# First mixture-of-experts layer computed over groups of 3, 3, 4 and 3 token tiles, with the first weights stationary

## Chip, cores, metric

The kernel runs on one core of one Trainium2 chip. The metric is the device time of one execution in microseconds (us). Before the change it is 708.86 us, the median of three runs (708.36 to 709.52).

## What is computed

Three layers follow each other. Attention over 2 x 8 heads of 768 tokens and width 64, masked by a hash bucket, gives 1536 tokens of width 512. Then a mixture of experts:

```python
logits = x @ w_gate + modality_bias[modality_id]      # x (1536, 512), 8 experts
e_idx = np.argmax(logits, axis=1)
gate_w = softmax(logits)[arange(N), e_idx]
for e in range(E):
    mask = e_idx == e
    h = np.maximum(x[mask] @ w1[e], 0.0)              # w1 (8, 512, 1024)
    out[mask] = gate_w[mask, None] * (h @ w2[e])      # w2 (8, 1024, 512)
```

and a second layer `h = x @ w_in; g = max(h,0) + alpha*min(h,0); g @ w_out` with inner width 2048, called the second mixture here. Everything is 32-bit. The matrix products of both mixtures are done in three terms: each operand is split into a rounded high part and the rest (high x high, rest x high, high x rest).

## The kernel before, in words

The order of every instruction is written out by hand; each engine runs its own list in that order.

**Routing.** The 768 tokens of the first batch are routed while attention still runs. Their most frequent expert fills three tiles of 128 tokens (`NPRE = 3`) ahead of time. The rest of the routing (`Router.S`, `R`, `adjust`, `GATE`, `place`, `experts`, `tokens`, `slots`, `slots2`), a row of small VectorE operations, runs after attention, between the matrix products of those first three tiles. `experts` writes the expert of each tile, whether it differs from the tile before, and the number of tiles. 13 tiles (`NBASE`) are always computed; tiles beyond are computed in `rest`, under a branch on the number.

**One tile t.** `TX` transposes the 128 gathered tokens (4 TensorE transposes) and splits them into high and rest (one ScalarE and one VectorE operation). `G1` makes two halves of 128 tokens x 512 hidden columns: the tokens are stationary, the weights `w1h`, `w1l` move, 12 matmuls of 512 columns a half; ScalarE evicts each half through a relu into `hr`. `TH` transposes the hidden tile (8 transposes) and splits it on ScalarE (`hh`) and VectorE (`hl`). `G2` makes 24 matmuls of 512 columns into `y`; `Y` scales by the gate on ScalarE and writes the tile to DRAM (`ys`). PSUM has 2 buffers for `G1` (`pg`), 3 for transposes (`ptr`), 2 for `y` and 1 for the router (`rps`).

**Weights.** SyncE loads the 4 MB of an expert for every tile (`load1`: `r1`, two halves of w1; `load2`: `r2`, w2). Where the expert changed, `W1s` and `W2` split them on ScalarE (high) and VectorE (rest), under a branch. For the first three tiles, the first layer's weights are split during the last steps of attention and those of the second layer by `W2()` after it.

**Around it.** `hook(s)` puts work between the attention steps: at step 96 tile 0 is transposed, at steps 98 and 100 the first half of its `G1` runs. During the main loop over tiles 3 to 12 the weights of the second mixture are loaded (`CL`) and repaired from 64-bit words (`CV`, five parts, the first on ScalarE, four on VectorE; all share one staging buffer), and the router's `dense`, `dense2` compute where each token's row lies in `ys`. At the end `GY` gathers rows of `ys`, `TY` transposes them, and the second mixture begins.

Of the kernel before, what the change touches and what calls it, by code (L numbers as in the profile page):

```python
# [35 lines left out]
LAGS = (0, 0)  # L36
ORDER = "aVDNmbnefopAL"
# [7 lines left out]
NBASE = 13  # L45
ELD = 88
# [8 lines left out]
class Router:  # L55
# [5 lines left out]
    def constants(self, w_gate, mbias, mod):  # L61
# [60 lines left out]
        yield  # L122

# [257 lines left out]
    def experts(self):  # L381
# [12 lines left out]
        v.tensor_tensor(out=a, in0=a, in1=self.iota[0:1, 0:8].unsqueeze(1).to_broadcast(s), op=ALU.mult)  # L394
        et = self.tmp([1, NT], F32, "et")
        v.tensor_reduce(out=et, in_=a, axis=AX.X, op=ALU.add)
        v.tensor_copy(et[:, 0:NPRE], self.es[0:1].to_broadcast([1, NPRE]))
# [3 lines left out]
        tt = self.tmp([1, 1], F32, "ttt")  # L401
        v.tensor_reduce(out=tt, in_=nt[0:1, 0], axis=AX.X, op=ALU.add)
        v.tensor_scalar(out=info[:, 2 * NT:2 * NT + 1], in0=tt, scalar1=float(NPRE), scalar2=None, op0=ALU.add)
# [52 lines left out]
    def dense2(self, ps):  # L456
        nc = self.nc
        v = nc.vector
        HD, rv = self.dn
        p = ps()  # L460
        for c in range(12):
            nc.tensor.matmul(p[:, 0:36], HD[:, c], rv[:, c].rearrange("p a t -> p (a t)"), start=(c == 0), stop=(c == 11))
        t = self.tmp([128, 3, 12], F32, "dt")
        v.tensor_copy(t, p[:, 0:36].rearrange("p (a t) -> p a t", a=3))
        v.tensor_copy(self.did, t[:, 0])
        v.scalar_tensor_tensor(out=self.dpos, in0=t[:, 2], scalar=128.0, in1=t[:, 1], op0=ALU.mult, op1=ALU.add)
# [7 lines left out]
def _program(base, tc, nc, q, k, v, proj, mod, w_gate, mbias, w1, w2, win, wout, alpha, out):  # L474
# [6 lines left out]
    ys = dram.tile([NT * 128, 512], F32, tag="ys", name="ys")  # L481
# [21 lines left out]
    def hook(s):  # L503
# [11 lines left out]
        if 74 <= s < 74 + NT - NBASE:  # L515
            t = NBASE + s - 74
# [34 lines left out]
        if s == 96:  # L551
            z = slot16(0)
            h, lo = R["x0"] = z[:, 0:512], z[:, 512:1024]
            p = misc()
            for kk in range(4):
                nc.tensor.transpose(p[:, kk * 128:kk * 128 + 128], xg[0][:, kk * 128:kk * 128 + 128], ident)
            nc.scalar.activation(h, p, AF.Copy)
            nc.vector.tensor_tensor(out=lo, in0=p, in1=f32(h), op=ALU.subtract)
        if s in (98, 100):
            h, lo = R["x0"]  # L560
            w1h, w1l = R["w1"]
            if s == 98:
                R["g0"] = GP()
            p = R["g0"]
            for kk in range(s - 98, s - 96):
                ks = slice(kk * 128, kk * 128 + 128)
                for n, (a, b) in enumerate(((h, w1h), (lo, w1h), (h, w1l))):
                    nc.tensor.matmul(p, a[:, ks], b[:, kk, 0:512], start=(kk == 0 and n == 0), stop=(kk == 3 and n == 2))
            if s == 100:
                R["hr0"] = BIG[0][:, 1536:2048]  # L570
                nc.scalar.activation(R["hr0"], p, AF.Relu)
# [395 lines left out]
    def rps():  # L967
        return prt.tile([128, 512], F32, tag="rps", name="rps")

    def trp():  # L970
        return ptr.tile([128, 512], F32, tag="tr", name="tr")

# [30 lines left out]
    xhl, hr, hhl, yps, gps = {0: R["x0"]}, {}, {}, {}, {}  # L1003

    def TX(t):
        p = ptr.tile([128, 512], F32, tag="tr", name="tr")
        for kk in range(4):
            nc.tensor.transpose(p[:, kk * 128:kk * 128 + 128], xg[t][:, kk * 128:kk * 128 + 128], ident)
        if t < NBASE:
            h = mp.tile([128, 512], F32R, tag="xh", name="xh", bufs=2)  # L1010
            lo = mp.tile([128, 512], F32R, tag="xl", name="xl", bufs=2)
        else:
            h, lo = R["xr"][:, 0], R["xr"][:, 1]
        act.activation(h, p, AF.Copy)
        dve.tensor_tensor(out=lo, in0=p, in1=f32(h), op=ALU.subtract)
        xhl[t] = (h, lo)

    def G1(t, half, k0=0, k1=4):
        h, lo = xhl[t]
        if half == 0 and k0 == 0:  # L1020
            h_ = mp.tile([128, 1024], F32, tag="hr", name="hr", bufs=2)
            hr[t] = h_[:, 0:512], h_[:, 512:1024]
        hs = slice(half * 512, half * 512 + 512)
        if k0 == 0:
            gps[t] = pg.tile([128, 512], F32, tag="g", name="g")
        p = gps[t]
        for kk in range(k0, k1):
            ks = slice(kk * 128, kk * 128 + 128)
            for n, (a, b) in enumerate(((h, w1h), (lo, w1h), (h, w1l))):
# [476 lines left out]
```

## Time and profile before

| | |
|---|---|
| median of three runs | 708.86 us |
| the profiled execution, device time | 711.61 us |
| its span, first to last instruction | 709.8 us |
| TensorE busy | 676.0 us, 95% |
| VectorE busy | 443.1 us, 62% |
| ScalarE busy | 331.8 us, 47% |
| mean granted TensorE clock | 0.982 of 2.4 GHz |

PE is TensorE's matmul, PEld its weight load, DVE is VectorE, ACT ScalarE, POOL GpSimd, SP SyncE. L1030 is line 1030 of the kernel. A matmul's duration contains its latency, and the next one begins before it ends; what a matmul costs in a row of them is the distance from start to start. Time in microseconds unless marked ns; clock times are counted from the start of the span. Attention ends at about 258 us, the first mixture at 429 us.

### The profile page before, as it was taken

Reading aid. Unit: us, or ns where it says so; the run is one execution under the profiler, and the core shown is the slowest. Engines: PE = TensorE matmul, PEld = TensorE weight load, DVE = VectorE, ACT = ScalarE, POOL = GpSimd, SP = SyncE. Lnnn points to the kernel's source line nnn. Section 1 sums busy time; section 2 is a strip of 40 time slices with the busy share of each in tenths; the row PEclk is TensorE's granted clock in tenths of the full one; section 3 lists DMA queues with packets and bytes.
Section 4 is the critical chain, followed back from the end, with each engine's and each line's share of the span. In section 5 each row is a group of like instructions: output and inputs, shape, how many; then the busy total and the mean of one; then the engine's idle time right before and its main releaser. Section 6 shows DMA issues by size and latency. Waiting matters only on the chain. (4 is left out here: it accounts for less than half of the span.)

```text
span 709.8 us, 13037 instructions
## 1 busy us (share of the span) xinstructions
PE 676.0 (95%) x4970; PEld 562.3 (79%) x4970; DVE 443.1 (62%) x905; ACT 331.8 (47%) x561; POOL 237.2 (33%) x208
## 2 busy tenths in 40 slices
PE   7799999999989889999999989999999999999996
PEld 6588898998878768788888767788888888888884
DVE  6878788889887768316724557999643344434332
ACT  5577687787867754234533337666311111111111
POOL 8777889998857400210100022021021000110002
PEclk9989999999999899999999999999999999999999
DMA  8375863874624141316522374443011010010001
GB/s 211 92 192 120 187 157 77 182 216 93 136 98 169 43 162 62 109 30 247 199 90 75 89 259 147 128 134 133 1 46 44 1 30 0 16 44 1 1 0 59
DMA packets 31420, 72.41 MB, mean 102 GB/s; under 512 B 7116, under 2 KB 7206, under 8 KB 31094
## 3 DMA queue, kind: packets, MB, share of 16 engines
q1 hardware_dynamic: 28260, 61.81, 30.9%
q0 software_dynamic: 2960, 9.70, 4.1%
q8 instruction: 40, 0.66, 0.4%
q14 instruction: 30, 0.25, 0.1%
q10 hardware_dynamic: 130, 0.00, 0.0%
HBM read 79.15 MB, written 12.06 MB: 128 GB/s over the span
## 5 line engine op out<-in xcount | busy, mean ns | idle before, releaser
L836 POOL TENSOR_TENSOR El<-E,Eh 128x768 f16<-128x768 f32 x88 | 144.4, 1652 | 40.0 <-ACT Eh L835 21.5
L831 ACT ACTIVATE E<-st 128x384 f32<-128x384 f32 x192 | 89.2, 491 | 61.2 <-PE st L830 57.5
L798 DVE TENSOR_REDUCE mx<-mxp 128x1 f32<-128x384 f32 x192 | 97.6, 547 | 10.5 <-PE mxp L797 9.7
L585 ACT ACTIVATE gh<-gf 128x512 fp32r<-128x512 f32 x48 | 30.3, 630 | 143.9 <-PE o L1351 133.4
L835 ACT ACTIVATE Eh<-E 128x768 f16<-128x768 f32 x94 | 79.5, 846 | 0.0
L829 PE MATMUL st<-op 97*128 97x384 f32 x192 | 74.8, 389 | 2.5 <-DMA op<-mr 1.9
L797 PE MATMUL mxp<-op 76*128 76x384 f32 x192 | 66.3, 359 | 6.9 <-ACT E L831 3.2
L588 DVE TENSOR_TENSOR gl<-gf,gh 128x512 fp32r<-128x512 f32 x48 | 33.1, 689 | 60.0 <-ACT gh L585 57.9
L1053 PE MATMUL y<-op,hh 128*128 128x512 f32 x208 | 69.7, 402 | 0.2 <-DVEq L1262 0.2
L1325 PE MATMUL h<-big,op 128*128 128x512 f32 x256 | 68.5, 396 | 0.0
L1368 POOL DMA_INDIRECT out_dram<-x,did x12 | 11.8, 985 | 169.2 <-DVE x L1365 89.8
L830 PE MATMUL st<-op 128*128 128x384 f32 x192 | 67.4, 351 | 0.0
L1351 PE MATMUL o<-op,gh 128*128 128x512 f32 x192 | 64.2, 395 | 0.0
L1030 PE MATMUL g<-op,xh 128*128 128x512 f32 x192 | 62.5, 397 | 1.1 <-PEq L1110 0.6
L846 PE MATMUL av<-vh,El 128*128 128x65 f16 x576 | 59.0, 196 | 2.0 <-POOL El L836 1.9
L844 PE MATMUL av<-vh,Eh 128*128 128x65 f16 x576 | 59.7, 197 | 0.0
L845 PE MATMUL av<-vl,Eh 128*128 128x64 f16 x576 | 59.2, 195 | 0.0
L844 PEld LDWEIGHTS <-Eh 128*128 128x128 f16 x576 | 53.1, 99 | 7.6 <-issue 6.4
L1325 PEld LDWEIGHTS h<-big,op 128*128 128x128 f32 x256 | 48.1, 188 | 11.6
L846 PEld LDWEIGHTS <-El 128*128 128x128 f16 x576 | 53.7, 99 | 2.2 <-POOL El L836 2.2
L845 PEld LDWEIGHTS <-Eh 128*128 128x128 f16 x576 | 53.8, 100 | 0.0
L1207 POOL DMA_INDIRECT yg<-ys,dpos x10 | 12.9, 1287 | 120.6 <-DVE x L1163 65.4
(406 smaller groups left out, 1502.2 us busy)
## 6 DMA issues: line engine op xcount, KB each, us to landing
r<-in_moe_w_dram SPq DMA_DIRECT2D x42, 1024.0 KB
op<-B SPq DMA_DIRECT2D x32, 192.0 KB
op<-in_moe_w_in_dram SPq DMA_DIRECT2D x6, 1024.0 KB
op<-A SPq DMA_DIRECT2D x28, 192.0 KB
op<-A SPq DMA_DIRECT2D x13, 384.0 KB
op<-in_moe_w_out_dram SPq DMA_DIRECT2D x4, 1024.0 KB
ys<-ysb SPq DMA_DIRECT2D x13, 256.0 KB
big<-in_q_dram SPq DMA_DIRECT2D x17, 192.0 KB
```

The lines of the kernel that those rows point to most:

```text
L797: mm(p[:,0:384],t[0:76,2,c*128:(c+1)*128],t[0:76,1,a*384:a*384+384],start=True,stop=True)
L798: nc.vector.tensor_reduce(out=mx[h][:,c,a:a+1],in_=p[:,0:384],axis=AX.X,op=ALU.max)
L829: mm(p[:,0:384],t[0:97,1,js],t[0:97,2,qs],start=True,stop=False)
L830: mm(p[:,0:384],t[:,0,js],t[:,3,qs],start=False,stop=True)
L831: nc.scalar.activation(E[s][0][:,qs],p[:,0:384],AF.Exp,scale=0.125)
L835: else: nc.scalar.activation(eh,e,AF.Copy)
L836: (nc.vector if s>=ELD else nc.gpsimd).tensor_tensor(out=el,in0=e,in1=eh,op=ALU.subtract)
L844: mm(a[:,c*65:c*65+65],eh[:,cs],VH[h//4%2][:,j,h%4,:],start=(j==0 and c==0),stop=False,skip_group_check=True)
L845: mm(a[:,c*65:c*65+64],eh[:,cs],VL[h//4%2][:,j,h%4,:],start=False,stop=False,skip_group_check=True)
L846: mm(a[:,c*65:c*65+65],el[:,cs],VH[h//4%2][:,j,h%4,:],start=False,stop=False,skip_group_check=True)
L1053: nc.tensor.matmul(yps[t], a[:, ks], b[:, kk], start=(kk == 0 and n == 0), stop=(kk == 7 and n == 2))
L1325: nc.tensor.matmul(p, terms[t][0][:, kk, cs], terms[t][1][:, kk], start=(n == 0), stop=(n == 11))
```

## The change

The 13 tiles become four groups of 3, 3, 4 and 3. In a group, `G1(key, c)` makes one chunk of 128 hidden columns for all the group's tokens: 128 columns of w1 are stationary, the tokens move (384 or 512 columns), 12 matmuls a chunk, 8 chunks. Its output has the hidden columns on the partitions already, so `TH` goes. ScalarE evicts the chunk through a relu as high part, VectorE makes the rest from the same PSUM tile. `G2(key, c)` adds one chunk to all the group's `y`. `Y` alternates between ScalarE and VectorE. PSUM: 2 buffers for `G1`, 4 for `y`, 2 for transposes and router together.

The expert's weights are loaded once for a group. `experts` works on 128 partitions and adds six operations that tell whether every group has one expert and the tiles are at most 13; if not, all tiles after the third go through `rest` one by one, into other rows of `ys`. At attention's end three tiles are transposed (steps 96, 97) and the first chunk of group 0 is computed (steps 99, 100). The main loop is a list of 24 chunks, each followed by the second layer of the chunk two before; weight splits, `CL`, `CV`, gathers are hung on numbered chunks. `ys` is cleared with 19 writes of 256 KB rather than 9.

```diff
+HB = 4
+GROUPS = ((0, 1, 2), (3, 4, 5), (6, 7, 8, 9), (10, 11, 12))
+NG = NT - NPRE
...
+        self.wt = P([128, NT], F32, "wt")
+        nc.gpsimd.memset(self.wt, 0.0)
...
         info = self.info = self.pp.tile([1, 2 * NT + 1], I32, tag="info", name="info")
-        v.tensor_copy(info[:, 0:NT], et)
-        v.tensor_tensor(out=info[:, NT + 1:2 * NT], in0=et[:, 1:NT], in1=et[:, 0:NT - 1], op=ALU.not_equal)
...
+        v.tensor_copy(info[:, 0:NT], et[0:1])
+        ne = self.tmp([128, NT], F32, "ne")
+        v.tensor_tensor(out=ne[:, 1:NT], in0=et[:, 1:NT], in1=et[:, 0:NT - 1], op=ALU.not_equal)
+        v.tensor_copy(info[:, NT + 1:2 * NT], ne[0:1, 1:NT])
+        tt = self.tmp([128, 1], F32, "ttt")
+        v.tensor_reduce(out=tt, in_=nt[:, 0], axis=AX.X, op=ALU.add)
+        v.tensor_scalar(out=tt, in0=tt, scalar1=float(NPRE), scalar2=None, op0=ALU.add)
+        lt = self.tmp([128, NT], F32, "lt")
+        v.scalar_tensor_tensor(out=lt, in0=it, scalar=tt, in1=self.wt, op0=ALU.is_lt, op1=ALU.mult)
+        v.tensor_tensor(out=ne[:, 1:NT], in0=ne[:, 1:NT], in1=lt[:, 1:NT], op=ALU.mult)
+        irr = self.irr = self.tmp([128, 1], F32, "irr")
+        v.tensor_reduce(out=irr, in_=ne[:, 1:NT], axis=AX.X, op=ALU.max)
+        v.scalar_tensor_tensor(out=irr, in0=tt, scalar=float(NBASE), in1=irr, op0=ALU.is_gt, op1=ALU.max)
+        v.tensor_tensor(out=info[:, 2 * NT:2 * NT + 1], in0=tt[0:1], in1=irr[0:1], op=ALU.mult)
...
-        if 74 <= s < 74 + NT - NBASE:
+        if 64 <= s < 64 + NG:
...
+        if s in (96, 97):
...
+            for t in ((0, 1), (2,))[s - 96]:
+                TX0(t)
+        if s in (99, 100):
...
+                for n, (w, x) in enumerate(((w1h, hi), (w1h, lo), (w1l, hi))):
+                    nc.tensor.matmul(p, w[:, kk, 0:128], x[:, kk], start=(kk == 0 and n == 0), stop=(kk == 3 and n == 2))
             if s == 100:
+                h, lo = R["h0"] = R["zx"][:, 3072:3456], R["zx"][:, 3456:3840]
+                nc.scalar.activation(h, p, AF.Relu)
+                nc.vector.scalar_tensor_tensor(out=lo, in0=p, scalar=0.0, in1=f32(h), op0=ALU.max, op1=ALU.subtract)
...
-    ptr = psB.enter_context(tc.tile_pool(name="ptr", bufs=3, space=PSUM))
-    py = psB.enter_context(tc.tile_pool(name="py", bufs=2, space=PSUM))
-    prt = psB.enter_context(tc.tile_pool(name="prt", bufs=1, space=PSUM))
+    py = psB.enter_context(tc.tile_pool(name="py", bufs=4, space=PSUM))
+    ptr = psB.enter_context(tc.tile_pool(name="ptr", bufs=2, space=PSUM))
...
+    def G1(key, c):
+        hi, lo, n = XT[key]
+        p = pg.tile([128, 512], F32, tag="g", name="g")[:, 0:n]
+        cs = slice(c * 128, c * 128 + 128)
+        for kk in range(4):
+            for m, (w, x) in enumerate(((w1h, hi), (w1h, lo), (w1l, hi))):
+                nc.tensor.matmul(p, w[:, kk, cs], x[:, kk], start=(kk == 0 and m == 0), stop=(kk == 3 and m == 2))
...
+        act.activation(h, p, AF.Relu)
+        dve.scalar_tensor_tensor(out=lo, in0=p, scalar=0.0, in1=f32(h), op0=ALU.max, op1=ALU.subtract)
+
+    def G2(key, c):
...
+        for i in range(n):
+            ts = slice(i * 128, i * 128 + 128)
+            for m, (a, w) in enumerate(((h, w2h), (lo, w2h), (h, w2l))):
+                nc.tensor.matmul(yps[key][i], a[:, ts], w[:, c], start=(c == 0 and m == 0), stop=(c == 7 and m == 2))
...
+    G1(0, 1)
     rr.L(1, 3, 0, rps)
     rr.L(1, 3, 1, rps)
     run(rr.S(1, rps))
...
+    G1(0, 2)
+    W2(0, 1)
+    G1(0, 3)
     run(rr.R(1, rps))
...
     run(rr.adjust(1, rps))
+    G1(0, 4)
+    W2(1, 2)
     rr.GATE(1, rps)
...
     rr.place()
+    rr.experts()
+    G1(0, 5)
+    W2(2, 3)
     rr.tokens()
+    G1(0, 6)
     rr.slots()
+    W2(3, 4)
+    G1(0, 7)
...
+    G2(0, 0)
+    G2(0, 1)
     rr.slots2(rps)
+    for t in GROUPS[1]:
+        GA(t)
+    G2(0, 2)
+    G2(0, 3)
...
+        G2(0, 4)
+        TX(1, 3, 0)
+        G2(0, 5)
+        TX(1, 4, 1)
+        G2(0, 6)
+        TX(1, 5, 2)
+        G2(0, 7)
+    Ys(0)
...
+    for p, q in ((4, 3), (3, 0), (0, 1), (1, 2), (2, 6), (6, None), (5, None)):
+        fs += CVs(p)
+        if q is not None:
+            fs[-1] = lambda p=p, q=q: (CV(p, 4), CL(q))
+    for k, n in ((4, 2), (5, 3), (7, 2), (9, 1), (10, 2), (12, 2), (13, 3), (14, 2), (16, 3), (17, 3), (18, 2), (19, 3), (20, 2), (21, 3), (22, 2)):
+        on(end, k, *fs[:n])
+        del fs[:n]
...
+    for k in range(26):
+        if k == 16:
+            G2(*order[14])
+        if k < 24:
+            G1(*order[k])
+        for f in mid.get(k, []):
+            f()
...
+        if k >= 2 and k != 16:
+            G2(*order[k - 2])
+            if order[k - 2][1] == 7:
+                Ys(order[k - 2][0])
...
+        for f in end.get(k, []):
+            f()
```

## Rows read from the trace of the kernel before

**Rows 1.** The page: engine totals; a costly group with the idle time before it.
```profile
PE 676.0 (95%) x4970; PEld 562.3 (79%) x4970; DVE 443.1 (62%) x905; ACT 331.8 (47%) x561; POOL 237.2 (33%) x208
...
L829 PE MATMUL st<-op 97*128 97x384 f32 x192 | 74.8, 389 | 2.5 <-DMA op<-mr 1.9
```
**Rows 2.** Busy time by stretch: stretch, length, engines' busy us, granted clock, DMA share, GB/s.
```profile
258.50:297.00 38.50, 37.85 (x221) 31.45 (x222) 25.04 (x76) 14.47 (x24) 3.80 (x4) 1.00 0.36 124
297.00:429.00 132.00, 128.08 (x626) 103.68 (x625) 62.24 (x84) 51.92 (x79) 10.94 (x10) 1.00 0.43 147
429.00:500.00 71.00, 69.94 (x299) 55.72 (x299) 65.35 (x77) 46.38 (x64) 10.91 (x5) 1.00 0.37 123
```
**Rows 3.** Timeline of PE in G1 of a tile: start, length, instruction; three matmuls apart.
```profile
300.05 0.62 PE L1030 MATMUL g<-op,xh 128*128 128x512 f32 x2
...
300.74 0.62 PE L1030 MATMUL g<-op,xh 128*128 128x512 f32 x2
```
**Rows 4.** Timeline of PE in attention, matmuls of 384 columns; four apart.
```profile
235.26 0.34 PE L829 MATMUL st<-op 97*128 97x384 f32 x1
...
235.97 0.34 PE L829 MATMUL st<-op 97*128 97x384 f32 x1
```
**Rows 5.** One line's instructions, weight loads of G1: ns min/median/max, first and last start.
```profile
L1030 PEld LDWEIGHTS g<-op,xh x192: 186/188/190, 265.5 to 417.0; 128*128 128x128 f32 x192
```
**Rows 6.** Timeline of PE: four transposes between two matmuls of G2.
```profile
427.23 0.60 PE L1219 MATMUL tr<-ident,yg 128*128 128x128 f32 x4
427.59 0.48 PE L1053 MATMUL y<-op,hh 128*128 128x512 f32 x1
```
**Rows 7.** Groups by shape on PE, TH's transposes: busy us, mean ns, idle before.
```profile
L1041 PE MATMUL tr<-ident,hr 128*128 128x128 f32 x100 | 13.3, 274 | 0.5 <-ACT hr L1032 0.5
```
**Rows 8.** Timeline of ACT: split of w2 after attention, idle time and releaser in brackets.
```profile
266.31 1.06 ACT L585 ACTIVATE op<-r 128x1024 fp32r<-128x1024 f32 x1 [0.26 <-DMA r<-in_moe_w_dram]
```
**Rows 9.** Timeline of DVE: w2's split, then first operations of the router's parts.
```profile
266.08 5.21 DVE L588 TENSOR_TENSOR op<-r,op 128x1024 fp32r<-128x1024 f32 x4 [0.84 <-ACT op L585]
...
273.64 0.17 DVE L324 COPY rps<-e 128x6 f32<-128x6 f32 x1
...
276.85 0.21 DVE L222 TENSOR_REDUCE rps<-ex 128x6 f32<-128x48 f32 x1
...
278.16 0.17 DVE L228 TENSOR_TENSOR vals<-rps,vals 128x6 f16<-128x6 f32 x1
...
280.44 0.16 DVE L367 TENSOR_TENSOR nt<-cnt,selm 128x8 f32<-128x8 f32 x1
...
282.20 0.36 DVE L409 TENSOR_TENSOR tkp<-oh,sd 128x192 f32<-128x192 f16 x1
...
285.05 0.15 DVE L386 TENSOR_TENSOR en<-sd,nt 1x8 f32<-1x8 f32 x1
...
287.44 0.16 DVE L271 CAST ids<-rps 128x22 int32<-128x22 f32 x1
```
**Rows 10.** Groups by shape on DVE: a difference of 384 columns from PSUM.
```profile
L728 DVE TENSOR_TENSOR vl<-misc,vh 128x384 f16<-128x384 f32 x16 | 8.9, 558 | 0.6
```
**Rows 11.** Timeline of PE at the end of the first mixture: two waits.
```profile
420.12 0.50 PE L1053 MATMUL y<-op,hl 128*128 128x512 f32 x1 [0.88 <-DVE hl L1044]
...
424.92 0.63 PE L1219 MATMUL tr<-ident,yg 128*128 128x128 f32 x4 [0.73 <-DMA yg<-ys,dpos]
```
**Rows 12.** Busy time by stretch near attention's end: a gap of PE, then a stretch of clock 0.50.
```profile
236.00:239.00 3.00, 1.12 (x24) 0.85 (x23) 2.16 (x3) 3.00 (x8) 2.91 (x2) 1.00 0.29 83
241.00:247.00 6.00, 6.00 (x64) 5.51 (x65) 5.11 (x11) 2.39 (x6) 0.00 (x0) 0.50 0.01 3
```
**Rows 13.** Timeline of SP: issue of the two w1 halves of a tile, 1 MB each.
```profile
320.88 1.15 SPq L598 DMA_DIRECT2D r<-in_moe_w_dram  x2
```
**Rows 14.** Timeline of ACT: the split of those halves, each waiting for its load.
```profile
326.06 2.01 ACT L585 ACTIVATE op<-r 128x1024 fp32r<-128x1024 f32 x2 [0.61 <-DMA r<-in_moe_w_dram]
328.76 2.01 ACT L585 ACTIVATE op<-r 128x1024 fp32r<-128x1024 f32 x2 [0.70 <-DMA r<-in_moe_w_dram]
```

More of the change, by code (lines that the diff above doesn't have):

```diff
@@ L965, in run @@
             pass
[L967 to L968 removed]
     def trp():
         return ptr.tile([128, 512], F32, tag="tr", name="tr")
+    rps = trp
     def W1s(halves=(0, 1)):
@@ L1018, in G1 @@
[L1018 to L1029, printed above, removed]
-                nc.tensor.matmul(p, a[:, ks], b[:, kk, hs], start=(kk == 0 and n == 0), stop=(kk == 3 and n == 2))
-        if k1 == 4:
-            act.activation(hr[t][half], p, AF.Relu)
@@ L1127, in rest @@
                 W2()
-    R["xr"] = big(1, (128, 2, 512), F32R)
-    rest(NBASE)
-    Y(2)
+    xr = mp.tile([128, 4096], F32R, tag="xt", name="xr")
+    XT["r"] = cols(xr, 128), cols(xr[:, 512:1024], 128), 128
+    rest(NPRE)
     BIG[2] = big(2)
@@ L1278, in _program, with CVs, first @@
-    CV(5, 0)
-    CV(5, 1)
-    CV(5, 2)
-    G1(last, 1)
-    for n in range(4):
-        GY(n)
-    TH(last)
-    CV(5, 3)
-    CV(5, 4)
-    CL(LP[1])
-    for i in range(3):
-        wslot(i)
-    G2(last, 0, 4)
-    TY(0, ptr)
-    TY(1, ptr)
-    G2(last, 4, 5)
-    SP(0, 0)
-    SP(0, 1, "D")
-    TY(2, ptr)
-    G2(last, 5, 6)
-    TY(3, ptr)
-    G2(last, 6, 8)
-    Y(last)
+    def CVs(p):
+        return [lambda i=i: CV(p, i) for i in range(5)]
+    def first(g, hs):
+        with changed(GROUPS[g][0]):
+            W1s(hs)
@@ new lines, in second, with early, newx, late @@
+    def second(g, n0, n1):
+        with changed(GROUPS[g][0]):
+            W2(n0, n1)
+    def early(g, w):
+        t = GROUPS[g][0]
+        if t not in er:
+            er[t] = reg(t, 7), reg(NT + t, 1)
+        load(t, er[t][0], which=(w,))
+    def newx(g):
+        a = mp.tile([128, 4096], F32R, tag="xt", name="xt")
+        n = 128 * len(GROUPS[g])
+        XT[g] = cols(a, n), cols(a[:, 2048:4096], n), n
+    def late():
+        global_ = R["x34"] = [R["rp"].tile([128, 2048], F32, tag=f"r1{i}", name=f"x{i + 3}") for i in range(2)]
+        a, b = global_
+        cb[6] = (x2[:, 0:2048].bitcast(I32), b[:, 0:1024])
+        cb[5] = (a.bitcast(I32), b[:, 1024:2048])
@@ new lines, in rest_of, with on @@
+    def rest_of():
+        x3 = R["x34"][0]
+        for n, p in enumerate(LP):
+            cb[p] = (x3, x2, BIG[2])[RW[n]][:, 0:2048].bitcast(I32), (BIG[2], x2)[n % 2][:, 2048:3072] if n < 8 else x3[:, 1024:2048]
+    cb[6] = (x2[:, 0:2048].bitcast(I32), None)
+    order = [(g, c) for g in (1, 2, 3) for c in range(8)]
+    mid, end = {}, {}
+    def on(d, k, *fs):
+        d.setdefault(k, []).extend(fs)
+    on(end, 0, lambda: CL(4), lambda: early(2, 1), lambda: GA(6), lambda: GA(7), rr.dense)
@@ new lines, in _program @@
+    on(end, 1, lambda: early(2, 2), lambda: GA(8), lambda: GA(9), lambda: newx(2))
+    for i, t in enumerate(GROUPS[2]):
+        on(mid, 2 + i, lambda t=t, i=i: TX(2, t, i))
+    on(end, 3, lambda: rr.dense2(rps))
+    on(end, 6, lambda: first(2, (0,)))
+    on(mid, 8, lambda: first(2, (1,)))
+    on(end, 8, lambda: second(2, 0, 2))
+    on(end, 9, lambda: early(3, 1))
+    on(end, 10, lambda: second(2, 2, 4), lambda: GA(10), lambda: GA(11), lambda: GA(12))
+    on(end, 11, lambda: early(3, 2))
```

256 lines of the change are left out of this document (98 added, 158 removed).

## Prediction

> **What bounds the kernel now.** I read the page first: TensorE is busy 95% of the span, no other engine over 62% [rows 1]. Then the stretches the change touches. From 258.5 to 297 (the three early tiles with the rest of the routing) TensorE idles 0.65 us of 38.5; from 297 to 429 (the loop over ten tiles) 3.9 us of 132; the clock is 1.00, that is 2.4 GHz, in both [rows 2]. So the first mixture ends when TensorE's list ends, and TensorE work taken out of it is worth its full length unless another engine then comes last. VectorE is the candidate: in 258.5 to 297 it is busy 25.0 us, and nearly all of that lies before 288, where the router's last operations start [rows 2, 9]. Early in the second mixture it is busy 65.4 of 71 us [rows 2], but the change leaves that stage alone and moves its start with everything that feeds it.
>
> **Prices on TensorE.** Matmuls run into each other, so I take starts. Three of 512 columns lie 0.69 us apart, 0.230 each [rows 3]. Four of 384 columns lie 0.71 apart, 0.178 each [rows 4]: 0.46 ns a column against 0.45. Four transposes put between matmuls cost 0.36 us [rows 6].
>
> The weight load, 188 ns [rows 5], is longer than a 384-column matmul's 0.178, and still both fit: the load runs beside the matmuls before it. [...]
>
> **Part by part.** From 258.5 to 429 there are 170.5 us. *G1:* 312 matmuls of 512 columns (12 of them before 258.5) become 288 of 384 and 96 of 512 (12 of 384 before 258.5): 300 x 0.230 = 69.0 becomes 276 x 0.178 + 96 x 0.230 = 71.1, +2.1 us. *TH:* 104 transposes go. As 26 fours at 0.36 they are 9.4 us; by the busy time of the group, 13.3 for 100, at most 13.8 [rows 6, 7], but that contains the end of each burst, which lies beside the next matmul. I take 10.3: per tile one four at 0.36 and one at the inner distance, near 0.43. *TX:* two tiles' transposes move ahead of 258.5, -0.7 us. *G2* is unchanged, 312 x 0.230 = 71.8. The work by these prices is 159 us before (69.0, 10.3, 71.8, and 8 for token transposes and the router's small matmuls) and 150 after, **-8.9 us**; the 11 us over the work before are waits and small delays.
>
> *Before 258.5.* In steps 96 to 100 there are two more splits on ScalarE and VectorE, and VectorE's normalisation, which releases the attention output's write, comes some 0.6 us later. TensorE waits for the third split as it waits for the first one now. 12 matmuls get shorter by 0.6 us and eight transposes come in (0.7). I take 0.1 later in all, with -0.5 and +1 as the ends.
>
> *The early tiles on VectorE.* This is the costly part. Before, ScalarE alone evicted a half of `G1`, and TensorE could work ahead of VectorE. Now chunk c's PSUM buffer is free only when VectorE has made its rest, and `pg` has two buffers, so `G1(0,c)` waits for the rest of chunk c-2, which stands in VectorE's list behind the router. I follow that list. The first quarter of w2 can be split when its load lands. The second landed at 266.3 [rows 8]; the four split in 5.21, 1.3 each [rows 9], and if they land at that distance the first came at 265.0. It comes 0.6 later now, so ScalarE's part ends at 266.7 and VectorE's (a quarter of 5.21) at 268.0 [rows 9]. Then: rest of chunk 3 0.5 (an operation of that shape is 0.56, 0.5 from start to start in a row [rows 10]), three operations of `R` 0.6, `adjust` 273.64 to 276.85, 3.2; the rest of chunk 4 is done at 272.8. Then a quarter of w2 1.3, `GATE` 276.85 to 278.33, 1.5; `place` 280.44 to 282.20, 1.8; `experts` 285.05 to 287.44, 2.4, and its six new operations at 0.2, 1.2 [rows 9]; the rest of chunk 5 is done at 281.4. TensorE's side: from 258.6 the router's transposes and matmuls take 1.7 and chunks 1 to 7 2.14 each, so it would be through at 275.3. But chunk 6 starts at 272.8 and chunk 7 at 281.4, ending at 283.6: **+8.3 us**. Queued behind are only `G2(0,..)` and `slots2`, whose operands are ready by then; `GA` starts near 289.3 as it does now (288.4) and TensorE has three chunks of `G2` to cover the gathers. Ends: 6 if the w2 load is early or the operations on 128 partitions cost less, 10 if those of `experts` cost more.
>
> *The clock.* That gap leaves TensorE busy 2 us of 10. The nearest row is a gap of 1.9 us near 237, after which the clock was 0.50 (1.2 GHz) throughout 241 to 247, with TensorE busy before and during it [rows 12]. A stretch of 6 us at half rate does 3 us less work. Some of it will fall into the new gap itself, where it costs nothing, so I take **+2.5**, ends 0 and 5.
>
> *The waits.* Gone: those for `TH` and for the rows of `ys` at the end, 0.88 and 0.73 and two like them [rows 11], since the last tile's hidden transposes are gone and `TY` stands between chunks. Left: the branch waits, the same number on TensorE. Of the 11 us I keep half, **-5.6**; ends -3 and -8.
>
> *At nothing.* Weight loads fall from 4 MB a tile to 4 MB a group; the DMA share there is 0.36 and 0.43 [rows 2], so nothing waited for room. Splits for group 2 are spread over four chunks of 5.6 us with some 3 us of VectorE each; they stay hidden while `G1` has two chunks' lead. Ten more clearing writes pass through SyncE's queue in attention, and four clears through GpSimd's: their price is not in the trace; waits for the small DMA in that queue cost TensorE 1.9 us in all [rows 1], so they cost between -0.3 and +2, and I take +0.3, as that queue is seldom what TensorE waits for. The stage after 429 starts with ScalarE's last `Y` and the same splits behind it: no change.
>
> *Sum:* -8.9 + 8.3 + 2.5 - 5.6 + 0.1 + 0.3 = -3.3, on the profiled execution's 711.6 us. That one lies 2.7 above the median of the runs; the difference is carried to the median: 708.9 - 3.3 = **705.6 us**.
>
> **Rivals.** *VectorE's list does not hold TensorE.* If the router's operations move fast enough, or chunk 5's rest isn't what chunk 7 waits for, 8.3 and 2.5 go: 694.8 us. Against it stand the rows' durations; for it, that I know the list's lengths only from another order of work.
>
> *The gap costs more clock.* TensorE at 1.2 GHz through 13 of the 17 us of `G2(0,..)` loses 6.5 rather than 2.5: +4, 709.6 us, within 0.2% of now.
>
> *Slower: the conversions of the second mixture.* In chunks 16 to 22 a load `CL` is issued only when the conversion before it has ended on VectorE, and the next conversion's first part stands in ScalarE's list ahead of the relu that frees `G1`'s buffer. A 1 MB load landed 5.2 us after its issue (320.88 to 326.06), and 7.9 where it shared the queue [rows 13, 14]. At 5.2 chunk 22 waits 0.6 us by my layout, which the kept waits cover; beyond that each us of landing costs about two, since two such loads follow each other. At 7.9: +5.4, 711.0 us. It turns on the landing time, near 6.5 us. Against it: fewer weight loads share the engines.
>
> [...]
>
> *The general path.* If the groups mixed experts, ten tiles would be done again, each at no less than the 12 us of a tile now (a tenth of 132): over 820 us. The trace has the weights split once in the loop, just ahead of tile 6 [rows 14], so the expert changes at a border of the groups.
>
> **Chances.** Forecast 0.50, VectorE not holding 0.10, more clock 0.15, conversions 0.20, loads in line 0.03, general path 0.02. The range goes from 700.5 (transposes at their upper end, no clock loss, the gap at 6, partly offset) to 711.5 (the conversions, with the upper end of the attention cost). Differences under 0.2%, 1.4 us, can't be told from none here. Some of the forecast's own range lies within that: faster 0.53, same 0.23, slower 0.24.
>
> **What would show it.** TensorE's busy time falls by about 9 us; no hidden transposes; 384-column matmuls 0.178 apart. Two waits of TensorE between 270 and 282, the second near 6.5 us, released by VectorE, and a stretch of clock 0.50 behind it. VectorE's list without gaps from 266 to 288. Group 0 ending near 304, the first mixture near 425. The forecast is wrong if TensorE doesn't wait there, or if the relu in chunks 18 to 22 waits for a DMA.

## The result, and the profile after

The changed kernel takes 713.3 us (median of 20 runs, 708.2 to 716.8) against 708.73 for the kernel before on the same chip (20 runs): ratio 1.006, 95% interval 1.004 to 1.008. It is slower by 4 us, where 705.6 was forecast with a range of 700.5 to 711.5. The profiled execution took 716.79 us, its span is 715.0. Ratios here leave out executions over 1.5% slower than the fastest of their kernel, which medians keep; of e6 below these are five of twelve, the profiled one among them, so there the ratio is the one to read. The page of the profiled execution, engine totals, and TensorE's clock in 40 slices:

```profile
PE 670.8 (94%) x4938; PEld 569.8 (80%) x4938; DVE 447.6 (63%) x925; ACT 316.4 (44%) x536; POOL 236.6 (33%) x212
...
PEclk9879999999989899889999999999999999999998
```

TensorE's busy time fell by only 5.2 us [rows 1], and the mean clock from 0.982 to 0.963. To see where the time went I cut both traces at the same three events: attention's last product, the first `G1` matmul behind the three early tiles, and the first matmul of the second mixture. Busy time by stretch (columns as in [rows 2]), first before, then after:

```profile
256.10:298.00 41.90, 40.03 (x234) 32.56 (x230) 26.01 (x79) 15.09 (x25) 4.73 (x5) 1.00 0.36 123
298.00:429.10 131.10, 127.75 (x625) 103.70 (x626) 62.34 (x84) 51.92 (x79) 10.01 (x10) 1.00 0.43 147
```

```profile
257.20:311.50 54.30, 42.06 (x241) 36.71 (x238) 30.80 (x94) 13.51 (x23) 5.47 (x6) 0.93 0.52 181
311.50:435.70 124.20, 121.72 (x584) 105.30 (x585) 64.04 (x93) 37.78 (x56) 8.23 (x9) 0.96 0.52 180
...
283.60:290.40 6.80, 6.05 (x17) 5.67 (x18) 6.52 (x14) 0.49 (x1) 0.00 (x0) 0.50 0.83 284
310.90:317.70 6.80, 6.23 (x19) 6.24 (x20) 1.31 (x7) 0.49 (x1) 1.78 (x2) 0.50 0.80 262
413.30:416.70 3.40, 3.38 (x10) 2.88 (x11) 0.00 (x0) 0.00 (x0) 0.96 (x2) 0.50 1.00 361
```

The early part became 12.4 us longer, the ten tiles 6.9 us shorter; the second mixture, from its first to its last matmul, took 272.4 us instead of 273.9. The DMA share rose from 0.36 and 0.43 to 0.52 in both parts, where a fall of the loads was forecast (see *Why the prediction was wrong*). The last three rows are three new stretches at a clock of 0.50. In the first, twelve matmuls of 384 columns take 4.01 us (284.35 to 288.36), where at 1.00 they take 2.11 (404.12 to 406.23). In the second they start 0.320 us apart, 1.2 columns a ns; the prediction's 1.2 GHz is this rate, if a column takes a cycle (an estimate). Half of TensorE's busy time in the stretches is my estimate of the price: 3.0, 3.1 and 1.7 us, 7.8 in all. Each stands behind a wait. The waits, in the timeline of PE (start, length, instruction, count, idle time before it and its releaser):

```profile
271.75 3.28 PE L1051 MATMUL g<-op,op 128*128 128x384 f32 x18
276.01 2.38 PE L1051 MATMUL g<-op,op 128*128 128x384 f32 x12 [0.98 <-DVE h L1058]
284.35 1.97 PE L1051 MATMUL g<-op,op 128*128 128x384 f32 x5 [5.96 <-DVE h L1058]
...
307.52 0.40 PE L1068 MATMUL y<-op,hh 128*128 128x512 f32 x1
311.47 7.79 PE L1051 MATMUL g<-big,op 128*128 128x384 f32 x27 [3.55 <-ACTq L1135]
...
404.12 2.27 PE L1051 MATMUL g<-xt,op 128*128 128x384 f32 x12
406.23 0.39 PE L1068 MATMUL y<-op,hh 128*128 128x512 f32 x1
...
408.90 2.36 PE L1051 MATMUL g<-xt,op 128*128 128x384 f32 x12 [0.42 <-DVE hl L1058]
413.32 1.09 PE L1242 MATMUL tr<-ident,yg 128*128 128x128 f32 x4 [2.06 <-DMA yg<-ys,dpos]
```

The first two are the waits for VectorE's list that were forecast. The third, 3.55 us, stands at the hand-over from group 0 to group 1; L1135 is the branch for the rest of the tiles. Before, TensorE lost 0.56 + 0.54 us at that branch, and ScalarE's last `Y` ran behind it, not ahead of it (PE, then ACT, of before):

```profile
297.02 0.39 PE L1053 MATMUL y<-op,hh 128*128 128x512 f32 x1
297.97 0.50 PE L1030 MATMUL g<-op,xh 128*128 128x512 f32 x1 [0.56 <-PEq L1110]
...
299.25 0.73 PE L1030 MATMUL g<-op,xh 128*128 128x512 f32 x2 [0.54 <-DVEq L1110]
```

```profile
298.07 0.69 ACT L1058 ACTIVATE ysb<-y,gp 128x512 f32<-128x512 f32 x1 [2.83 <-PEq L1110]
```

After, the change has put `Ys(0)` ahead of the branches. Its last eviction on ScalarE waits for TensorE's last `G2` matmul (307.52), runs to 308.64, and only then can ScalarE go through the two branches that stand there; TensorE's next matmul, 2.83 us later, waits for that (ACT, then DVE, of after):

```profile
306.55 0.69 ACT L1076 ACTIVATE ysb<-y,gp 128x512 f32<-128x512 f32 x1
307.95 0.69 ACT L1076 ACTIVATE ysb<-y,gp 128x512 f32<-128x512 f32 x1 [0.71 <-PE y L1068]
```

```profile
307.25 0.75 DVE L1074 TENSOR_SCALAR ysb<-y,gp 128x512 f32<-128x512 f32 x1
```

The last wait is at the end of the loop. The four rows of `ys` of group 2 are issued between two 1 MB loads of the second mixture, the gathers begin 9 us after that issue, and ScalarE meanwhile waits twice for such loads (SP, POOL and ACT of after):

```profile
399.79 0.38 SPq L1173 DMA_DIRECT2D op<-in_moe_w_in_dram  x1
400.27 2.55 SPq L1077 DMA_DIRECT2D ys<-ysb  x4
402.87 0.49 SPq L1173 DMA_DIRECT2D x<-in_moe_w_out_dram  x1
```

```profile
409.44 1.35 POOL L1230 DMA_INDIRECT yg<-ys,dpos  x1 [77.33 <-DVE hl L1058]
```

```profile
405.80 1.13 ACT L1180 ACTIVATE big<-op 128x1024 f32<-128x1024 f32 x1 [5.67 <-DMA op<-in_moe_w_in_dram]
...
419.06 1.15 ACT L1180 ACTIVATE x<-op 128x1024 f32<-128x1024 f32 x1 [11.37 <-DMA op<-in_moe_w_in_dram]
```

So there were three candidates for the loss: the place of `Ys(0)`, the gap in group 0 with its low clock, and the end of the loop; a fourth, the ten added clearing writes in attention, can't be read from one trace.

### The profile page after: what moved, and what is told of

Its sections match the earlier page's. It is cut to its first block, busy times and chain, and to the rows that moved or that the text cites. A ratio compares the mean times of both kernels' runs of the same rounds, so it can differ in the third digit from the quotient of the medians.

```text
span 715.0 us, 12760 instructions
## 1 busy us (share of the span) xinstructions
PE 670.8 (94%) x4938; PEld 569.8 (80%) x4938; DVE 447.6 (63%) x925; ACT 316.4 (44%) x536; POOL 236.6 (33%) x212
## 5 line engine op out<-in xcount | busy, mean ns | idle before, releaser
L828 DVE TENSOR_REDUCE mx<-mxp 128x1 f32<-128x384 f32 x192 | 97.7, 547 | 12.6 <-PE mxp L827 11.8
L1406 POOL DMA_INDIRECT out_dram<-x,did x12 | 11.8, 988 | 167.8 <-DVE x L1403 89.1
L1068 PE MATMUL y<-op,hh 128*128 128x512 f32 x172 | 59.8, 406 | 0.0
L1363 PE MATMUL h<-big,wp 128*128 128x512 f32 x192 | 51.4, 394 | 0.0
```

Source lines behind the costliest of these rows:

```text
L828: nc.vector.tensor_reduce(out=mx[h][:,c,a:a+1],in_=p[:,0:384],axis=AX.X,op=ALU.max)
L1068: nc.tensor.matmul(yps[key][i], a[:, ts], w[:, c], start=(c == 0 and m == 0), stop=(c == 7 and m == 2))
L1363: nc.tensor.matmul(p, terms[t][0][:, kk, cs], terms[t][1][:, kk], start=(n == 0), stop=(n == 11))
```

## Experiments

All are kernels of their own, each timed against the kernel before on its own chip. "Early part" and "ten tiles" are the two stretches cut as above, in one profiled execution; "hand-over" is TensorE's wait there.

| kernel | median us | ratio to before, 95% interval | early part | ten tiles | hand-over |
|---|---|---|---|---|---|
| before | 708.7 to 709.8 | 1 | 41.9 | 131.1 | 1.10 |
| changed | 713.30 | 1.0060 [1.0037, 1.0082] | 54.3 | 124.2 | 3.55 |
| e1, `Ys(0)` behind the branch | 707.16 | 0.9971 [0.9946, 0.9996] | 51.8 | 121.6 | 2.11 |
| e7, before with `Y(2)` ahead of the branch | 714.10 | 1.0059 [1.0031, 1.0087] | 46.1 | 132.8 | 4.69 |
| e11, e1 with one branch moved | 707.21 | 0.9978 [0.9950, 1.0006] | 51.9 | 122.2 | 2.18 |
| e12, changed with one branch moved | 711.72 | 1.0042 [1.0013, 1.0071] | 54.2 | 123.3 | 3.48 |
| e2, second layer fills the gap | 710.23 | 1.0024 [0.9998, 1.0049] | 54.7 | 123.1 | 5.28 |
| e6, idle matmuls fill the gap | 712.79 | 1.0017 [0.9982, 1.0051] | 52.5 | 129.7 | 3.56 |
| e4, before with 19 clearing writes | 710.20 | 1.0018 [0.9996, 1.0039] | 42.7 | 130.6 | 1.29 |
| e3, `TY` a chunk later | 714.22 | 1.0062 [1.0025, 1.0099] | 54.2 | 127.4 | 3.63 |
| e9, conversions earlier | 711.48 | 1.0026 [0.9997, 1.0055] | 53.0 | 122.9 | 3.54 |
| e8, e1 + e9 + group 0 reordered | 705.59 | 0.9960 [0.9930, 0.9990] | 45.2 | 124.1 | 2.99 |
| e10, e8 + `TY` later + one branch moved | 701.15 | 0.9889 [0.9846, 0.9932] | 45.1 | 124.1 | 2.95 |
| e13, e8 + `TY` later | 701.55 | 0.9894 [0.9857, 0.9930] | 45.3 | 122.7 | 3.04 |

### The hand-over

e1 moves `Ys(0)`; for that the skipped general path takes another PSUM buffer for its `y`. Nothing else changes.

```diff
-    Ys(0)
     with changed(NPRE):
         W2()
...
     rest(NPRE)
+    Ys(0)
```

> The changed kernel with one step moved: the three evictions of group 0 (Ys(0)) come after the skipped branches of `changed` and `rest`, as the last tile's did in the kernel before (the general path's own y takes a transpose buffer instead). Theory A: ScalarE reaches its branches only after it has evicted tiles that wait for TensorE's last matmul, and TensorE's first matmul of group 1 waits for ScalarE to be past them. Then the idle time of 3.6 us at 307.5 falls to about 1 us, the clock stays at full rate behind it, and the time falls by 5 to 6 us, to some 707.5. Rival B: the branch costs this by itself, for the skipped code is 19 levels now and was 9. Then the wait stays above 3 us and the time within 1 us of the changed kernel's 713.3.

707.16 us: 6.1 under the changed kernel, and below the kernel before. The wait fell to 2.11 us, and the low clock behind it to half. Of the 5.1 us by which the two stretches of its profile are shorter, these are 1.44 and 1.4; another 0.7 and 1.7 are less low clock at the gap in group 0 and at the gathers, which the edit does not touch (PE; busy time by stretch):

```profile
306.07 2.14 PE L1051 MATMUL g<-big,op 128*128 128x384 f32 x6 [2.11 <-DVEq L1134]
```

```profile
306.10:309.50 3.40, 3.40 (x11) 3.40 (x12) 0.75 (x1) 0.31 (x1) 2.32 (x3) 0.52 0.86 255
```

The counter-experiment, e7, is the kernel before with only this order taken from the change.

```diff
         G2(2, 4, 8)
+    Y(2)
...
     rest(NBASE)
-    Y(2)
```

> The kernel before with one step moved as the change moves it: the eviction of tile 2 (Y(2)) stands ahead of the branch of `rest` instead of behind it. Theory A: ScalarE then gets to its branch only after TensorE's last matmul of tile 2, and TensorE waits for it: the waits at 297 to 299, 1.1 us now, grow to 2.5 to 4, and the time by 1.5 to 4 us with the clock behind it. Rival B (what counts is the longer code that is skipped): waits and time as in the kernel before, within 0.2%.

One moved line made the kernel before slower by 5 us, to 714.1, more than the 1.5 to 4 that were expected. Its wait at the branch is longer than the changed kernel's, and a stretch at 0.50 follows here too, 300.4 to 303.8 (PE, ACT):

```profile
300.87 0.80 PE L1030 MATMUL g<-op,xh 128*128 128x512 f32 x1 [4.69 <-ACTq L1111]
```

```profile
296.26 0.69 ACT L1058 ACTIVATE ysb<-y,gp 128x512 f32<-128x512 f32 x1 [2.25 <-PEq L1111]
```

ScalarE's eviction ends at 296.95 and TensorE goes on at 300.87: the eviction itself takes 0.69 us, and 3.9 us pass behind it (2.83 in the changed kernel). What costs is less the eviction than ScalarE's pass of the branch, which the order brings behind TensorE's last matmul.

Why 2.11 us and not 1? Two branches stand there. e11 (from e1) and e12 (from the changed kernel) move the one around `W2()` behind the first chunk of group 1.

```diff
-    with changed(NPRE):
-        W2()
...
-    on(end, 0, lambda: CL(4), ...
+    on(end, 0, lambda: second(1, 0, 4), lambda: CL(4), ...
```

> The changed kernel with two edits: Ys(0) stands behind the branch for the rest of a group's tiles (as in the run that moved it alone, 707.16 us), and the branch around the split of the group's second weights moves behind the first chunk of group 1, so that only one of the two branches stands between the groups. Theory A1 (each branch that stands at the hand-over is a wait of its own, since the work queued ahead of it on VectorE has to end before it is passed): TensorE's wait there falls from 2.1 to at most 1.2 us, the low clock behind it shrinks, and the time falls by 1 to 3 us, to 704 to 706. Theory A2 (the wait is set by VectorE's splits of the last token transposes alone, and the second branch costs nothing): wait about 2 us as before, time 706.5 to 708.

> The changed kernel with the branch around the split of the second weights moved behind the first chunk of group 1, and Ys(0) left where the change puts it, ahead of the branch for the rest. Theory A (Ys(0), which waits for TensorE's last second-layer matmul, ahead of any branch is the price): the wait at the hand-over stays over 3 us, time 712 to 714. Theory A1 (two branches rather than one are the price): the wait falls to 1 to 2.5 us, time 707 to 710.

Neither wait changed (2.18 and 3.48 us, both still released at the branch for the rest), so the second branch is not the price. A2's number came true in e11; its reason did not, for in e8 below VectorE is idle and the wait is 2.99 us. e12's median, 711.72, lies just under the 712 to 714 of the first theory and above the 707 to 710 of the other; the wait decides. The order of `Ys(0)` and the branch is the cause of the larger part, shown in both directions; what sets the 2 us that are left is open (below). That the skipped `rest` is 19 levels deep where it was 9 (rival B) is a candidate for it that no run takes alone.

### The gap in group 0

e2 moves three chunks of `G2` ahead of `G1(0,7)` and a fourth right behind it, so that TensorE has work while VectorE's list runs; group 1's token transposes come one chunk later.

```diff
     W2(3, 4)
+    G2(0, 0)
+    G2(0, 1)
+    G2(0, 2)
     G1(0, 7)
+    G2(0, 3)
```

> The changed kernel with four chunks of group 0's second layer moved on TensorE's list: three ahead of chunk 7 of the first layer, one ahead of the slot matmuls; the three token transposes of group 1 one chunk later. VectorE's list is the same. Theory A: TensorE waits in group 0 because chunk 6 and 7 need PSUM buffers that VectorE frees late; other work that is ready can stand there. The waits of 1.0 and 6.0 us near 275 and 278 fall to about 1 in all, the stretch of clock 0.50 at 283.5 goes, group 0 ends 8 to 9 us earlier, and the time falls to about 705. Rival C: the routing itself bounds the stage; then most of the wait comes back where the gathered tokens are transposed or the slots are multiplied, and the time falls by less than 4 us.

The wait of 5.96 us went, the early part stayed at 54.7 us and the median fell by 3 us, as rival C has it: two other waits took its place (PE; SP and POOL of the same kernel):

```profile
296.50 1.09 PE L1039 MATMUL tr<-ident,xg 128*128 128x128 f32 x4 [4.75 <-DMA xg<-x_d,ids]
...
310.17 2.26 PE L1051 MATMUL g<-big,op 128*128 128x384 f32 x6 [5.28 <-DVEq L1135]
```

```profile
283.24 5.19 SPq L631 DMA_DIRECT2D r<-in_moe_w_dram  x2
```

```profile
289.42 0.97 POOL L642 DMA_INDIRECT xg<-x_d,ids  x1 [48.73 <-DVE gc L285]
```

The gathers of group 1's tokens can only start when the router is through (the operation that releases them starts at 289.15), behind 4 MB of weights issued from 281.98 on. TensorE reached their transposes at 291.75 and waited for them until 296.50. Why the wait at the hand-over grew to 5.28 us is not shown. In the changed kernel these gathers were hidden by the `G2` chunks behind the gap.

e6 leaves VectorE's list as it is and puts 32 matmuls of 384 columns into the gap, whose result nobody reads.

> The changed kernel with 32 matmuls of 384 columns (0.178 us each, 5.7 in all) on TensorE's list in front of chunk 7 of group 0; they write an unused buffer, nothing reads it, and they fill the wait of 6.0 us there. Everything else is as it was. Theory A: a long wait costs more than its length, for the clock falls behind it; then the stretch of 0.50 near 283 goes, group 0's second layer takes 17 us instead of 19.5, and the time falls by about 2.5 us though no wait was removed. Rival G: the half rate there has another cause; then it stays and the time is the changed kernel's.

TensorE was busy through the gap (0.43 us idle left), and no stretch at 0.50 followed it: the clock is 1.00 throughout 268 to 290 (PE; busy time by stretch):

```profile
273.23 5.71 PE L1107 MATMUL idl<-op,op 128*128 128x384 f32 x32
279.37 2.35 PE L1051 MATMUL g<-op,op 128*128 128x384 f32 x12 [0.43 <-DVE h L1058]
```

```profile
268.00:290.00 22.00, 20.55 (x115) 18.32 (x114) 16.96 (x59) 4.78 (x7) 2.01 (x3) 1.00 0.46 168
```

The early part fell by 1.8 us, of the 3.0 that the low clock costs there; 1.10 came back as a wait for gathers. At the end of the loop this execution waits 6.78 us for gathers, so its ten tiles take 129.7. In the ratio e6 and the changed kernel can't be told apart: their intervals overlap.

### Attention

e4 is the kernel before with 19 clearing writes instead of 9 in SyncE's queue.

> The kernel before with one part of the change alone: 19 clearing writes of 256 KB from step 64, instead of 9 from step 74. Theory E: these writes slow attention, which ended 3.2 us later in the profile after; then this kernel is 1 to 3 us slower than the one before, 710 to 712. Rival F: attention's end moves from execution to execution and the writes cost nothing that can be measured; then the ratio is 1 within 0.2%.

+0.18%, interval from -0.04% to +0.39%: at most 2.8 us, and no cost at all is inside. The +0.3 that was taken lies inside.

### The end of the loop

e3 puts `TY`, the transposes of the gathered rows, one chunk later.

> The changed kernel with the transposes TY of the four gathered tiles one chunk later each (21 to 24 instead of 20 to 23). Theory A: the gather of ys starts 6 us late because group 2's tiles are written behind 1 MB loads of the second mixture on the same DMA engines; TensorE's wait of 2.1 us at 411 and the half clock from 413.3 to 416.7 come from it. With one more chunk of cover the wait goes, and the time falls by 2 to 4 us, to about 710. Rival D: the tail is held by ScalarE's wait for the load of conversion 6; then the wait turns up at a relu or a split instead, and the time stays within 1 us of 713.3.

The time stayed, as rival D has it (714.22 us). The wait for the gathers went, and a longer one came at nearly the same place: ScalarE's first part of a conversion, which waits for its load, stands ahead of the relu whose rest TensorE needs (PE, ACT):

```profile
417.64 3.92 PE L1051 MATMUL g<-xt,op 128*128 128x384 f32 x12 [5.15 <-DVE hl L1058]
```

```profile
414.55 1.12 ACT L1180 ACTIVATE x<-op 128x1024 f32<-128x1024 f32 x1 [12.38 <-DMA op<-in_moe_w_in_dram]
```

e9 takes the conversions earlier instead, spread from chunk 2 on, and the load `CL(5)` two chunks later.

```diff
-    for k, n in ((4, 2), (5, 3), (7, 2), (9, 1), (10, 2), ...
+    for k, n in ((2, 2), (3, 3), (5, 2), (6, 3), (9, 2), ...
```

> The changed kernel with the five-part conversions of the second mixture's weights hung on earlier chunks (the first at 2 and 3 instead of 4 and 5, the sixth at 18 and 19 instead of 19 and 20), so that each load has one chunk or more to itself, and the load of conversion 5 two chunks later, behind the gathers. Theory D: the waits at the end, whether at the gathered tokens (2.1 us) or at a rest that VectorE makes late (5.2 us where the gathered tokens' turn came later), come from three 1 MB loads, group 2's tiles and the gathers meeting on the DMA engines between 400 and 416. Then ScalarE's waits for loads (5.7 and 11.4 us) shrink below 4, TensorE's waits between 400 and 420 fall from 2.5 to under 1, and the time falls by 2 to 4 us. Rival H: the waits come from the conversions' length on VectorE alone; then they stay near 2.

The waits for `hl` went; the one for the gathers grew to 3.00 us, and the median fell by 1.8 where 2 to 4 were expected:

```profile
405.48 1.09 PE L1242 MATMUL tr<-ident,yg 128*128 128x128 f32 x4 [3.00 <-DMA yg<-ys,dpos]
```

Each of the two alone uncovers the other's wait. That they only pay together is what the last group of runs asks.

### All together

e8 takes e1 and e9 and reorders group 0: the router's `tokens` and `slots` come straight after `place`, `experts` and the weights' load behind them, three chunks of `G2` ahead of `slots2`. e10 adds e3's later `TY` and e11's moved branch; e13 adds the later `TY` alone. The reorder of group 0, its new places only:

```diff
     rr.place()
+    rr.tokens()
+    rr.slots()
     G1(0, 5)
     G1(0, 6)
+    G2(0, 0)
+    G2(0, 1)
+    G2(0, 2)
+    rr.slots2(rps)
+    for t in GROUPS[1]:
+        GA(t)
     W2(2, 3)
+    G2(0, 3)
+    rr.experts()
+    G1(0, 7)
     W2(3, 4)
```

> The changed kernel with the evictions of group 0 behind the branches, the conversions earlier, and group 0 in another order: `tokens` and `slots` directly behind `place`, `experts` and with it the load of the next expert behind the slot matmuls and the gathers, three chunks of the second layer ahead of the slot matmuls, chunk 7 behind them, the token transposes of group 1 ahead of the last two chunks of the second layer. Theory A with C and D (the first group is bound by the router's list and the gathers behind it, the gathers by the 4 MB load that shares the engines; the end by the loads): group 0 ends near 297 instead of 307.5, its waits are under 4 us in all, and the time is 694 to 698. If the branches cost their 3 us wherever they stand, 697 to 701. If group 0's waits only move again, above 703.

> The version with all mended (Ys(0) late, group 0's router work and first second-layer chunks reordered, conversions earlier: 705.59 us) with two more edits: the second weights' branch behind the first chunk of group 1, and the transposes of the gathered tokens one chunk later. The earlier run left a wait of 2.99 us at the hand-over with 6.9 us at the low clock, and one of 3.1 us for the gathered tokens with 3.5 us at the low clock. If both are set by what these edits move: 2 us less wait and 3 us less low clock at the first place, 3 and 1.7 us at the second, so 698 to 701. If VectorE's list at the tail cannot hold one more chunk's delay (as the run that moved the transposes alone): the gain at the tail is lost again, 702 to 704.

> The version with all mended that gave 701.15 us, but with the branch around the split of the second weights left at the hand-over. Moving it had not shortened the wait there (2.95 us against 2.99) and had put a new one of 3.84 us behind the second chunk of group 1, with more of the low clock. If that new wait is the price of the moved branch: 1 to 5 us faster, 696 to 700. If the wait for Ys(0) behind the hand-over shows up in the same place with or without the branch (0.94 us of it in the earlier run): no faster than 700 to 702.

e8 gives 705.59 us, e10 and e13 701.15 and 701.55, the last two 1.1% under the kernel before. In e8 TensorE waits 0.97 and 0.56 us in group 0, and the early part is 45.2 us; but 2.99 us at the hand-over and 3.10 for the gathers are left, and the median is above the 694 to 698 that were expected (the profiled execution, 701.62, is the fastest of its twelve). e10 lies between its two expected ranges. With the conversions earlier, the later `TY` now pays 4 us in the median: e10 and e13 have no wait left at the end of the loop. The moved branch brought nothing: e10 has a wait of 3.84 us at that branch, e13 one of 2.53 at nearly the same place, both behind `Ys(0)`. What e13 has left in the two stretches (PE; DVE):

```profile
302.54 5.96 PE L1051 MATMUL g<-big,op 128*128 128x384 f32 x24 [3.04 <-DVEq L1134]
311.04 1.33 PE L1051 MATMUL g<-big,op 128*128 128x384 f32 x3 [2.53 <-DVE hl L1058]
```

```profile
295.96 0.69 DVE L1043 TENSOR_TENSOR big<-tr,big 128x512 fp32r<-128x512 f32 x1 [0.27 <-ACTq L1128]
309.29 0.75 DVE L1074 TENSOR_SCALAR ysb<-y,gp 128x512 f32<-128x512 f32 x1 [12.64 <-SPq L1134]
```

VectorE has had nothing to do since 296.65, and TensorE's last matmul ahead of the branch starts at 299.10; still VectorE's pass of the branch releases TensorE only at 302.5. `Ys(0)`, moved behind the branch, now waits for SyncE's pass of it, and holds the rests of group 1's first chunks.

## Why the prediction was wrong

In the profiled executions, from attention's end to the second mixture, the kernel went from 173.0 to 178.5 us, +5.5. The prediction's terms for that part sum to -3.6 (its +0.3 for the clearing writes belongs to attention). By its terms:

| term | predicted | measured | from |
|---|---|---|---|
| work, and waits other than those below | -8.9 - 5.6 + 0.1 = -14.4 | -11.7 | busy time less the clock's price, 167.8 to 156.0, and idle time +0.1 |
| group 0 behind VectorE's list | +8.3 | +6.9 | 0.98 + 5.96 |
| the clock | +2.5 | +7.8 | 3.0 + 3.1 + 1.7 |
| the branch at the hand-over | 0 | +2.5 | 3.55 less 1.10 |
| sum | -3.6 | +5.5 | |

**Right.** *Prices on TensorE:* twelve matmuls of 384 columns take 2.11 us (404.12 to 406.23), 0.176 each, where 0.178 was taken; the 188 ns weight loads stay hidden, for a load and a matmul in line would take 0.364. Already in [rows 3] matmuls start every 0.230 us, where in line with their loads [rows 5] they would need 0.418. So loads in line, 0.03 among the chances, are out. *The early tiles on VectorE:* two waits released by VectorE's rests, the second 5.96 us where 6.5 was worked out. Group 0 took 45.8 us from the router's first transposes to its end (261.7 to 307.5), against 45.5 from 258.5 to near 304. *The clock* behind that gap: 3.0 us against 2.5. That `GA` is covered by three chunks held too. The second mixture, put at nothing, gained 1.5 us that I did not trace.

**The step that failed** is *The waits*, in its clause that the branch waits stay "the same number on TensorE". I counted branches and did not follow the list of each engine up to them. Before, the last of the early tiles was scaled behind the branch; in a group all three end together, and the change scales them ahead of it; ScalarE's and VectorE's pass then begins after TensorE's last matmul instead of beside it. The price is 2.45 us of wait and 3.1 of low clock, 5.6 us. e7 makes the kernel before 5.0 slower by this order alone. e1 gives 6.1 back in the median, of which its profile shows 2.8 at this place and 2.4 as low clock elsewhere; the 2.11 us that it still waits are open.

**Also failed:** the same step's -5.6. It is half of 11 us taken for waits and small delays, of which [rows 2] show only 4.57 (0.65 and 3.92) as idle time of TensorE; in the first row of the table idle time changed by +0.1, and busy time fell by 11.8 where -8.9 was worked out.

The same step's claim that the waits at the end are gone since "`TY` stands between chunks" did not hold either. They went from the places in [rows 11] to a wait of 2.06 us for the gathers, with 1.7 us of low clock in this execution. *The rival of the conversions* named the right queue and the wrong victim: the loads landed in 6.0 us (399.79 to 405.80) and 7.8 (411.30 to 419.06), around its threshold of 6.5, but cost TensorE only 0.42 us at a chunk's rest. By the chain of the trace they cost more through the `ys` writes and gathers behind them, which *At nothing* put at nothing because the DMA share was 0.43 on the average of the stage. The last `ys` write took 6.25 us, and the share meanwhile reached 1.06 (chain that ended last; busy time by stretch); no run took a load away alone.

```profile
402.25 6.25 DMA ys<-ysb
...
409.44 3.74 DMA yg<-ys,dpos
```

```profile
405.80:409.40 3.60, 3.18 (x16) 2.44 (x15) 2.41 (x4) 1.89 (x3) 0.00 (x0) 1.00 1.06 418
```

*At nothing* also has the weight loads wrong, and with it the description of the kernel before. There a load has a condition, the flag that the expert changed; it is issued for every tile, and moves nothing where the expert stays. The change dropped the condition:

```diff
-            load(t + 1, *er[t + 1], which=(1,))
...
+    load(NPRE, er[NPRE][0])
...
+    load(t, er[t][0], which=(w,))
```

So the bytes that all queues move from attention's end to the second mixture did not fall but rose, from 24.4 to 32.2 MB. Before, eight loads of 1 MB are issued from 300 to 318, and all queues together move 0.82 MB; after, the four of group 1 from 283.5 to 300 are moved (DMA of before, then of after):

```profile
DMA packets 313, 0.82 MB, mean 46 GB/s; under 512 B 56, under 2 KB 56, under 8 KB 311
r<-in_moe_w_dram SPq DMA_DIRECT2D x8, 1024.0 KB
```

```profile
DMA packets 2301, 4.86 MB, mean 295 GB/s; under 512 B 96, under 2 KB 96, under 8 KB 2297
r<-in_moe_w_dram SPq DMA_DIRECT2D x4, 1024.0 KB
```

The weights of groups 1 and 3 are never split (ScalarE's splits in the loop, eight of 128x1024, one expert's, all lie between 340 and 361, for group 2): their experts are those of the groups before them, and their 8 MB make up the 7.8 MB more. The 4 MB issued ahead of the gathers in e2 are such weights. No run puts the condition back, so what it is worth is not shown.

**The size of the clock term** is the largest miss: 5.3 of 9.1 us. I priced it for one gap. In this execution the three waits of 2.06 to 5.96 us were each followed by 3.4 or 6.8 us at 0.50. For the shortest it is no certainty: e1, e2, e11 and e12 keep the wait for the gathers, 2.07 to 2.20 us, with the clock at 1.00 behind it. Of the 23 waits of 2.5 to 6.8 us between 250 and 440 us in all fourteen traces, 22 had such a stretch at or behind their end. The one without is e8's, 3.10 us for the gathers; behind it the clock is 1.00 (e10's expectation put 3.5 us of low clock there):

```profile
399.90:407.00 7.10, 7.10 (x38) 6.30 (x39) 2.05 (x4) 2.66 (x4) 0.95 (x1) 1.00 0.63 239
```

The upper end of the range was one rival alone; the hand-over and the end of the loop came together. e1, the forecast with most of its failed step undone, is at 707.2, inside it; the clock that differs elsewhere in its profile had a part in that.

## What to carry to other kernels

At a branch that all engines pass, write down for each engine the last instruction ahead of it and what that waits for; the engine whose list ends last adds to the wait, here 1.44 us (3.55 against 2.11, e1) and 3.59 (4.69 against 1.10, e7), and an operation that needs TensorE's last result belongs behind the branch. Price a new wait of TensorE with the low clock that follows it, here 1.5 to 3.1 us behind nearly every wait over 2.5 us and behind some of 2.1 to 2.2. Compare the bytes that each stage moves, not the loads written in the code: a load under a condition may move nothing (here eight of 1 MB were issued while all queues moved 0.82 MB). When filling a wait leaves the stage as long as before (e2, e3), look for the next late operand and move both: in e13 they paid together what neither had paid alone.

## What the runs showed of the hardware

*The price of a passed branch may depend on the DMA.* In e1 the wait at the hand-over is 2.11 us, in e8 2.99 with VectorE idle throughout. Busy time by stretch at that point, the DMA share and GB/s last, first e1, then e8:

```profile
303.00:306.00 3.00, 0.96 (x5) 0.42 (x3) 0.22 (x1) 0.85 (x2) 1.38 (x2) 1.00 0.08 14
```

```profile
291.00:296.40 5.40, 2.50 (x11) 1.69 (x9) 0.00 (x0) 0.00 (x0) 1.92 (x3) 0.92 1.05 377
```

and one of the DMA queues in the changed kernel from 308 to 312 (packets, MB, share of 16 engines):

```profile
q14 instruction: 3, 0.02, 1.5%
```

Three packets of the queue that the profile calls `instruction` move there, at a DMA share of 0.91. Whether the branch waits for them, no trace shows. With `Ys(0)` behind the branch the wait is longer where the DMA is full (e1, 0.08: 2.11 us; e8, e10 and e13, 1.04 to 1.05: 2.95 to 3.04), and in the last three VectorE and ScalarE have no work left to end (0.00 us busy). But the kernel before (1.10 us at 0.61) and e7 (4.69 us at 0.63) do not lie on one line with these, and no run took the DMA load away alone, so it is a reading and not shown.

*The same code ends attention at different times.* Its last product starts at 250.2 to 257.2 us in the eleven profiled executions with the changed attention, at 254.8 to 256.1 in the three with the old one, and the runs of one kernel spread by about 1%. Stretches at 0.50 within attention come and go between executions: e13's trace has them at 198 and 243, e8's has neither. This is as large as any single effect studied here; the stages cut at events of their own were needed to see them.
